# V's high part moved to ScalarE, the maximum turned in one pass, idle products, a tenth weight buffer and a new order of steps

## The chip, the core and the metric

The kernel runs on one core of a Trainium2 chip. The core has a matrix engine (TensorE, PE in the profile; its weight loads are PEld), three engines for elementwise work (VectorE is DVE, ScalarE is ACT, GpSimd is POOL) and SyncE (SP), which here only issues transfers. Every engine runs its own instructions strictly in the order in which they stand and waits for the others by semaphores. The metric is the device time of one launch in microseconds, as the median of several runs.

## The reference

Attention over 4 batches and 8 heads of 768 positions and 64 dimensions, in which a query sees the first 8 keys and the 96 keys up to itself, with a bias that falls linearly with the distance; then a soft mixture of 8 experts with 4 slots each over the 3072 resulting rows of 512.

```
scores = scale * q @ k.T + bias;  scores[~keep] = -1e9
a = softmax(scores);  x = (a @ v) as rows (B*S, H*D)
logits = x @ phi
slot_input = softmax(logits, over rows).T @ x
slot_out[e] = relu(slot_input[e] @ w1[e]) @ w2[e]
out = softmax(logits, over slots) @ slot_out
```

Everything is float32, and the weights w1 and w2 are 32 MB together.

## The kernel before

The attention is done in 16 units, numbered u: one pair of heads of one batch each. The keys of a unit stand in seven blocks of 120 (with the 8 global keys in front of each), and a block meets only the 216 queries that can see it. The code writes each stage of a unit as a small function, a step, and one long list, ORDER (line 51), says in which sequence the steps are issued. No scheduler comes after it: what ORDER gives is what every engine does in its queue. A step named `('w_lo', 3, 1, 2)` is w_lo of unit 3, head 1 of the pair, part 2.

The steps of a unit, with the lines of the kernel before:

- `load_qk` and `load_v` (L389, L392) fetch Q and K, and V. There are two buffers each.
- `scores(u, k)` (L518, PE) makes the products of Q and K in three parts, into two PSUM buffers sc used in turn; so a part can't start before the part two places ahead of it has been read.
- `biased(u, k)` (L527, DVE) reads such a part, adds the bias table and keeps the running maximum of each row.
- `max_t`, `max_r`, `max_b`, `max_c` (L534 PE, L537 DVE, L540 PE, L544 ACT) make one maximum of the unit out of the 128 of the rows and spread it again: a turn by a product with the identity, a reduction, a product, a copy.
- `exponential(u, i)` (L548, ACT) for the two heads i.
- `w_hi` (L551, ACT) rounds the weights to f16; `w_lo` in three parts (L558, POOL; a few as `w_lo_dve` on DVE) takes the difference to the rounded ones, also in f16. Each head has one buffer for them, so w_hi of the next unit waits until `values` of this one has read it.
- `v_hi` (L493, POOL) rounds V, scaled by 64, to f16, and `v_lo` (L500, DVE) makes the rest from V and v_hi.
- `values(u, i)` (L575, PE) makes 39 f16 products: high by high, high by low, low by high. It fills one half of the PSUM tile x.
- `ev_sums`, `ev_recs`, `ev_mul` (L588, L594, L600, DVE) divide by the row sums and free x; `tr` (L612, PE) turns the result and `tr_copy` (L617, ACT) copies it to SBUF; `logits` (L642, PE) follows after every second unit, and after every fourth the sums of the batch (`strip_...`, `by_token`, `dispatch`).

The bias table of the first pair is built by `table_even` and `table_odd` (L255 to L269, DVE), those of the other three by `table_pair` (L272, DVE). At the very start 12 products with a constant (L424) run on PE while nothing else can.

The weights come in 32 pieces of 1 MB. The first NW = 9 have buffers of their own and are loaded in the course of the attention (`piece`, and `extra` for parts of buffers that lie free). Thirteen more take the place of attention buffers as these fall free (`free`); the last ten are loaded once the first expert products have read theirs: five when the first half of the hidden products (L106) is issued, in halves, and five more in quarters. After the attention stand the last logits and sums, the hidden products (L106), their turning (L120), the combination weights (L170), the second products (L136, two output halves), and the combination (L196 to L202), which writes 12 times 512 KB.

## Time and profile before

| | |
|---|---|
| median of 3 runs | 218.66 us (218.41 to 218.75) |
| the profiled execution: its own time | 220.06 us |
| its span, from the first to the last instruction | 217.8 us |
| granted TensorE clock, mean | 0.933 |
| busy: PE, DVE, ACT, POOL | 183.6, 151.6, 121.4, 121.5 us |
| first `biased` starts | 10.04 us |
| `values` of unit 0, 2, 4, 12, first head, start | 27.87, 44.34, 59.25, 124.74 us |
| last `values` (unit 15, second head) ends | 151.34 us |
| last transfer to the output lands | 215.88 us |

The rows of a timeline read: start, duration, engine, line, operation, the tile written and the tiles read, and in brackets how long the engine had stood idle before and what ended that. A PE row covers several products, and its duration ends with the last of them; the next row starts some 0.07 to 0.16 us earlier than that, since products are pipelined.

### The profile page before, as it was taken

How to read it: one execution, taken by the hardware profiler on the slowest of the kernel's cores; microseconds unless marked ns; L12 is line 12 of the kernel's file. 1: busy time of each engine (PE TensorE's matmuls, PEld its weight loads, DVE VectorE, ACT ScalarE, POOL GpSimd, SP SyncE). 2: the span in 40 equal slices, each digit the busy share in tenths (PEclk: the TensorE clock that was granted, in tenths of full speed). 3: DMA queues.
4: the chain of work that ended last, by engine and by line, in shares of the span. 5: the costliest groups of instructions: out<-in, count | busy, mean ns of one | idle time of the engine just before them, and what ended most of it. 6: DMA issues, size and time to landing. Idle time of an engine off the chain costs nothing.

```text
span 217.8 us, 6430 instructions
## 1 busy us (share of the span) xinstructions
PE 183.6 (84%) x2644; PEld 135.3 (62%) x2644; DVE 151.6 (70%) x355; ACT 121.4 (56%) x169; POOL 121.5 (56%) x141
## 2 busy tenths in 40 slices
PE   8377799989898999998999998667899999899500
PEld 2155588878786787777787787456452366475500
DVE  4974759878878897988787997977367846151800
ACT  2008358598786786976886979962511653041500
POOL 7312929889999998898899799763000000000000
PEclk9955569999999999999999999999999999999965
DMA  4968429999998963755324657999985999979893
GB/s 149 414 248 307 161 86 354 377 377 399 389 385 311 343 232 125 242 175 196 120 75 169 225 166 246 416 381 389 369 331 178 409 409 387 386 270 342 280 339 123
DMA packets 21063, 61.40 MB, mean 282 GB/s; under 512 B 1952, under 2 KB 9376, under 8 KB 19488
## 3 DMA queue, kind: packets, MB, share of 16 engines
q1 hardware_dynamic: 20880, 60.89, 76.7%
q8 instruction: 23, 0.38, 0.7%
q14 instruction: 16, 0.13, 0.2%
q10 hardware_dynamic: 144, 0.00, 0.0%
HBM read 54.59 MB, written 6.29 MB: 280 GB/s over the span
## 4 chain that ended last, share of the span: by engine, by line
PE 41%; POOL 22%; DVE 15%; issue 10%; DMA 3%; ACT 3%; POOLq 0%; DVEq 0%; ACTq 0%; SPq 0%
POOL ph L558 20%; PE x L575 9%; PE x L136 7%; PE hp L106 6%; PE sc L518 6%; DVE ph L558 3%; DVE xn L600 2%; PE m L642 2%; PE m L612 2%; POOL v L493 2%; ACT ph L551 2%; DMA nraw<-in_n_dram 2%; DMA out_dram<-v 2%; DVE v L500 2%; PE ctp L170 2%
## 5 line engine op out<-in xcount | busy, mean ns | idle before, releaser
L558 POOL TENSOR_TENSOR ph<-tb,ph 128x432 f16<-128x432 f32 x91 | 101.4, 1147 | 21.5 <-ACT ph L551 21.1
L518 PE MATMUL sc<-raw 64*128 64x216 f32 (+2 forms) x448 | 53.6, 372 | 5.2 <-DVE mx L527 4.7
L551 ACT CAST ph<-tb 128x1296 f16<-128x1296 f32 x32 | 40.6, 1270 | 16.3 <-PE x L575 15.6
L575 PE MATMUL x<-v,ph 128*128 128x65 f16 (+1 forms) x1248 | 44.0, 195 | 6.5 <-DVE xmax L600 5.3
L518 PEld LDWEIGHTS sc<-raw 64*128 64x128 f32 x448 | 41.2, 206 | 13.0 <-DVE mx L527 6.2
L575 PEld LDWEIGHTS <-ph 128*128 128x128 f16 x1248 | 41.1, 98 | 12.5 <-issue 5.7
L548 ACT ACTIVATE tb<-tb,nb 128x1296 f32<-128x1296 f32 x32 | 43.5, 1375 | 0.3
L500 DVE SCALAR_TENSOR_TENSOR v<-vt,v 128x896 f16<-128x896 f32 x16 | 23.2, 1452 | 0.0
L527 DVE CUSTOM_DVE_ANT_1 tb<-sc,tt,mx 128x864 f32<-128x864 f32 x16 | 17.9, 1117 | 5.4 <-PE sc L518 4.8
L600 DVE CUSTOM_DVE_ANT_1 xn<-x,rc 120x448 f32<-120x448 f32 x32 | 18.9, 621 | 0.5
L493 POOL TENSOR_SCALAR v<-vt 128x896 f16<-128x896 f32 x16 | 15.7, 982 | 4.8 <-DVE mx L527 1.8
L612 PE MATMUL m<-ident,xn 120*128 120x120 f32 x105 | 15.4, 276 | 1.3 <-ACT xta L617 1.2
L544 ACT COPY nb<-m 128x1 f32<-128x1 f32 x16 | 2.6, 159 | 22.4 <-PE m L540 22.4
L612 PEld LDWEIGHTS m<-ident,xn 120*128 120x128 f32 x105 | 10.7, 141 | 3.5 <-ACT xta L617 1.4
L527 DVE CUSTOM_DVE_ANT_1 tb<-sc,tt 128x864 f32<-128x864 f32 x8 | 8.5, 1058 | 5.2 <-PE sc L518 4.8
L527 DVE CUSTOM_DVE_ANT_1 tb<-sc,xta,mx 128x864 f32<-128x864 f32 x8 | 8.9, 1118 | 2.4 <-PE sc L518 2.0
L106 PE MATMUL hp<-wp,sl 128*32 128x512 f32 x72 | 10.5, 594 | 0.0
L199 ACT COPY ph<-cp 128x512 f32<-128x512 f32 x8 | 4.1, 595 | 10.9 <-PE cp L196 10.9
L527 DVE CUSTOM_DVE_ANT_1 tb<-sc,xtt,mx 128x864 f32<-128x864 f32 x8 | 8.9, 1116 | 1.2 <-POOL v L493 0.6
L534 PE MATMUL m<-ident,mx 128*1 128x128 f32 x32 | 6.5, 286 | 2.5 <-DVE mx L527 2.5
L136 PE MATMUL x<-wp,tb 128*32 128x256 f32 x96 | 7.5, 381 | 1.1 <-DVE flag L858 1.1
L540 PEld LDWEIGHTS m<-mm,bsel 2*128 2x128 f32 x32 | 5.1, 198 | 4.8 <-DVE mm L537 1.2
(196 smaller groups left out, 272.3 us busy)
## 6 DMA issues: line engine op xcount, KB each, us to landing
raw<-in_qk_dram SPq DMA_DIRECT2D x15, 832.0 KB, 4.9
wp<-in_w_dram SPq DMA_DIRECT2D x9, 1024.0 KB, 9.2
vt<-in_v_dram SPq DMA_DIRECT2D x16, 448.0 KB, 4.7
wp<-in_w_dram SPq DMA_DIRECT2D x10, 512.0 KB, 7.5
out_dram<-ph SPq DMA_DIRECT2D x8, 512.0 KB, 5.2
tb<-in_w_dram SPq DMA_DIRECT2D x3, 1024.0 KB, 7.1
raw<-in_w_dram SPq DMA_DIRECT2D x8, 256.0 KB, 5.4
out_dram<-v SPq DMA_DIRECT2D x4, 512.0 KB, 6.1
```

The source lines that it names most:

```text
L106: nc.tensor.matmul(out=hp[n][32 * s:32 * s + 32, :], lhsT=slv(a, c, s), rhs=w1(e, c // 2)[:, (c % 2) * DF + 512 * n:(c % 2) * DF + 512 * n ...
L136: nc.tensor.matmul(out=o[32 * s:32 * s + 32, 0:w], lhsT=ht[:, c, 32 * s:32 * s + 32], rhs=w2(4 * a + s, half)[:, c0 + c * w:c0 + c * w + w ...
L493: nc.gpsimd.tensor_scalar(out=vhi[u % 2][:, :, :, 0:D], in0=vraw[u % 2], scalar1=V_SC, scalar2=0.0, op0=ALU.mult, op1=ALU.add)
L500: nc.vector.scalar_tensor_tensor(out=vlo[k].rearrange("p j i d -> p (j i) d"), in0=vraw[k].rearrange("p j i d -> p (j i) d"), scalar=V_SC, ...
L518: nc.tensor.matmul(out=z[:, i, at:at + n], lhsT=r_[r, KCOL[j]:KCOL[j] + KR], rhs=r_[r, KW + KB * j:KW + KB * j + n], start=True, stop=True)
L527: nc.vector.tensor_tensor_reduce(out=tb(u)[:, :, BW * k:BW * k + BW], in0=sc[(3 * u + k) % 2][:, :, 0:BW], in1=table.unit(u % NP, k), scal ...
L548: nc.scalar.activation(out=t, in_=t, func=AF.Exp, bias=nbs[u], scale=T_SC)
L551: nc.scalar.copy(out=blocks(phi_[i])[:, :, 0:QW], in_=tb(u)[:, i].rearrange("p (s c) -> p s c", c=QW))
L558: (engine or nc.gpsimd).tensor_tensor(out=blocks(plo_[i])[:, c, 0:QW], in0=tb(u)[:, i].rearrange("p (s c) -> p s c", c=QW)[:, c], in1=bloc ...
L575: nc.tensor.matmul(out=x[:, (D + 1) * t:(D + 1) * t + d], lhsT=w[:, c:c + P], rhs=vv[:, j, i, 0:d], start=(z == 0), stop=(z == len(ops) - ...
L600: nc.vector.tensor_tensor_reduce(out=xnb[(u // 2) % 3][:, :, c:c + D], in0=xv[:, i, :, 0:D], in1=rcs.pop((u, i)).unsqueeze(2).to_broadcast ...
L612: nc.tensor.transpose(out=m[:, at:at + KB], in_=xnb[(u // 2) % 3][:, t, P * (p % 2):P * (p % 2) + P], identity=ident[0:KB, 0:KB])
```

## The change

Five things change.

1. In 12 of the 16 units (all but 4, 7, 8 and 13) the step `v_hi` is replaced by `v_hi_act`, which does the same rounding on ScalarE: `nc.scalar.activation(out=vhi, in_=vraw, func=AF.Copy, scale=V_SC)`. The function stood in the kernel before and was not used.
2. `max_t` is a transpose of the column of 128 maxima (one pass of the array over the identity) in place of a product with the identity in float32.
3. A step `warm(u, count)` makes `count` products of a constant of ones with 512 columns, into the first row of x, which nobody reads. ORDER holds two: 7 after the scores (0, 1), and 10 after `max_b` of unit 0.
4. NW is 10. The tenth piece is loaded in the course of the attention, and of the ten late pieces nine remain (five in halves, four in quarters).
5. ORDER is another sequence throughout. Four `tr_copy` (of units 0, 5, 9 and 10) go to DVE, and four parts of w_lo in place of five: one of unit 9, three of unit 15, and none of unit 14.

```diff
-NW = 9
+NW = 10
-ORDER = [('load_qk0', 0), ('load_phis', 0), ('load_qk', 0), ('load_v', 0), ('keys', 0), ('load_qk', 1), ...
+ORDER = [('load_qk0', 0), ('load_qk', 0), ('load_v', 0), ('load_qk', 1), ('keys', 0), ('load_v', 1), ...
...
+    def warm(u, count):
+        for _ in range(count):
+            nc.tensor.matmul(out=xx[0:1, 0], lhsT=busy_in[:, 0:1], rhs=busy_in, start=True, stop=True)
...
     def max_t(u):
         ms[u, "m"] = m = bank(("max", u))
-        nc.tensor.matmul(out=m[0:1, 0:P], lhsT=mxs.pop(u)[:, 2:3], rhs=ident, start=True, stop=True)
+        nc.tensor.transpose(out=m[0:1, 0:P], in_=mxs.pop(u)[:, 2:3], identity=ident)
```

From the `warm` function on, the lines of the changed kernel stand four further down: the scores are L522 there, the maximum's turn L538, w_lo L562, the values L579.

The queue of PE from the first scores on, before. (sc_171 and sc_172 are the two score buffers, raw_92 and raw_93 Q and K of units 0 and 1.)

```order
L518 MATMUL sc_171<-raw_92 128x216 x4
L518 MATMUL sc_172<-raw_92 128x216 x4
L518 MATMUL sc_171<-raw_92 128x216 x2
L518 MATMUL sc_171<-raw_92 128x168 x2
L518 MATMUL sc_171<-raw_92 128x48 x2
L534 MATMUL m<-ident,mx 1x128
L518 MATMUL sc_171<-raw_93 128x216 x4
L540 MATMUL m<-mm_160,bsel 128x1
L518 MATMUL sc_172<-raw_93 128x216 x6
L518 MATMUL sc_172<-raw_93 128x168 x2
```

The same place now (all buffer numbers are higher by one; the weight loads of the idle products are left out, and their row L511, which stands seven times, is shown once):

```order
L522 MATMUL sc_172<-raw_93 128x216 x4
L522 MATMUL sc_173<-raw_93 128x216 x4
L511 MATMUL x<-const-bfloat16-1.0 1x512
L522 MATMUL sc_172<-raw_93 128x216 x2
L522 MATMUL sc_172<-raw_93 128x168 x2
L522 MATMUL sc_172<-raw_93 128x48 x2
L522 MATMUL sc_173<-raw_94 128x216 x4
L538 MATMUL m<-ident,mx 1x128
L522 MATMUL sc_172<-raw_94 128x216 x4
L544 MATMUL m<-mm_161,bsel 128x1
```

The first part of unit 1's scores now stands ahead of unit 0's maximum, and the seven idle products fill the place between the second and the third part of unit 0; ten more follow behind the last row shown.

The queue of POOL from its last constant to unit 2's second head, before (v_99 is V's f16 tile, ph_97 and ph_98 the weights' of the two heads):

```order
L443 MEMSET sl 128x280
L493 TENSOR_SCALAR v_99<-vt 128x14x64 x2
L558 TENSOR_TENSOR ph_97<-tb_94,ph_97 128x2x216 x3
L558 TENSOR_TENSOR ph_98<-tb_94,ph_98 128x2x216 x3
L558 TENSOR_TENSOR ph_97<-tb_95,ph_97 128x2x216 x3
L558 TENSOR_TENSOR ph_98<-tb_95,ph_98 128x2x216 x3
L493 TENSOR_SCALAR v_99<-vt 128x14x64
L558 TENSOR_TENSOR ph_97<-tb_96,ph_97 128x2x216 x3
L558 TENSOR_TENSOR ph_98<-tb_96,ph_98 128x2x216 x3
```

And now, to the second head of unit 3:

```order
L443 MEMSET sl 128x280
L562 TENSOR_TENSOR ph_98<-tb_95,ph_98 128x2x216 x3
L562 TENSOR_TENSOR ph_99<-tb_95,ph_99 128x2x216 x3
L562 TENSOR_TENSOR ph_98<-tb_96,ph_98 128x2x216 x3
L562 TENSOR_TENSOR ph_99<-tb_96,ph_99 128x2x216 x3
L562 TENSOR_TENSOR ph_98<-tb_97,ph_98 128x2x216 x3
L562 TENSOR_TENSOR ph_99<-tb_97,ph_99 128x2x216 x3
L562 TENSOR_TENSOR ph_98<-tb_95,ph_98 128x2x216 x3
L493 TENSOR_SCALAR v_100<-vt 128x14x64
L562 TENSOR_TENSOR ph_99<-tb_95,ph_99 128x2x216 x3
```

The first rounding of V left on POOL is that of unit 4. On ScalarE the queue now begins like this (L548 to L555 are L544 to L551 of before):

```order
L496 ACTIVATE v_100<-vt 128x14x64 x2
L548 COPY nb<-m 128x1
L552 ACTIVATE tb_95<-tb_95,nb 128x1296
L555 CAST ph_98<-tb_95 128x6x216
L552 ACTIVATE tb_95<-tb_95,nb 128x1296
L555 CAST ph_99<-tb_95 128x6x216
L548 COPY nb<-m 128x1
L552 ACTIVATE tb_96<-tb_96,nb 128x1296
L555 CAST ph_98<-tb_96 128x6x216
```

Two roundings of V stand ahead of the first exponential. Those of the later units stand mostly between the first exponential of a unit and its first rounding L555.

## The prediction

> **What bounds the kernel now.** I read the page first, then busy time by stage, the groups of instructions, and the timeline of the places that the stages point to. The page:

> ```profile
> span 217.8 us, 6430 instructions
> PE 183.6 (84%) x2644; PEld 135.3 (62%) x2644; DVE 151.6 (70%) x355; ACT 121.4 (56%) x169; POOL 121.5 (56%) x141
> PEclk9955569999999999999999999999999999999965
> ```

> The shares are means over stages of different kinds, and the clock row shows half speed in slices 3 to 5. So I cut the span where the clock changes and at values of units 2, 4 and 12 and the end of unit 15:

> ```profile
> core 0: us, PE busy (x) PEld busy (x) DVE busy (x) ACT busy (x) POOL busy (x), PEclk, DMA share, GB/s
> 4.26:11.09 6.83, 2.90 (x21) 1.54 (x19) 6.10 (x20) 0.00 (x0) 3.04 (x12) 1.00 1.04 405
> 11.09:31.57 20.48, 16.69 (x113) 12.99 (x115) 12.70 (x22) 9.43 (x9) 7.97 (x7) 0.50 0.59 209
> 31.57:44.34 12.77, 11.90 (x194) 10.05 (x193) 11.15 (x27) 8.03 (x10) 11.93 (x12) 1.00 0.89 331
> 44.34:59.25 14.91, 14.28 (x250) 12.15 (x251) 12.01 (x29) 12.33 (x17) 14.29 (x14) 1.00 0.99 392
> 59.25:124.74 65.49, 63.03 (x1053) 50.55 (x1053) 55.48 (x127) 51.68 (x70) 60.03 (x57) 1.00 0.63 217
> 124.74:151.34 26.60, 20.78 (x428) 17.68 (x429) 22.08 (x48) 18.82 (x24) 20.86 (x20) 1.00 0.86 321
> 151.34:217.80 66.46, 50.50 (x585) 29.20 (x584) 30.39 (x82) 19.60 (x40) 0.00 (x0) 0.93 0.88 318
> ```

> Four things are to be seen. From 11.09 to 31.57 us the clock is at 0.50 and POOL has only 7.97 us of work in 20.48. From 44.34 to 124.74 (ten units, 8.04 us each) PE is busy 77.3 of 80.4 us, so PE is the bound there and POOL (74.3) is close behind it. From 124.74 on no engine is full: a chain through all of them sets the pace. The last stage has nothing of the attention in it. The stage at half clock in the timeline:

> ```profile
> 0.77 4.46 PE L424 MATMUL wp<-const-bfloat16-1.0 128*1 128x512 bf16 x12 [0.77 <-PEq L1105]
> 6.63 1.00 PE L518 MATMUL sc<-raw 64*128 64x216 f32 x8 [0.47 <-DMA raw<-in_qk_dram]
> 8.00 1.35 POOL L493 TENSOR_SCALAR v<-vt 128x896 f16<-128x896 f32 x1 [1.71 <-DMA vt<-in_v_dram]
> 8.25 0.25 DVE L259 COPY tt<-xn 128x432 bf16<-128x432 bf16 x1
> 8.43 1.05 DVE L261 COPY tt<-xn 128x168 bf16<-128x168 bf16 x2
> 10.04 1.06 DVE L527 CUSTOM_DVE_ANT_1 tb<-sc,tt 128x864 f32<-128x864 f32 x1
> 11.16 1.95 PE L518 MATMUL sc<-raw 64*128 64x216 f32 x12 [3.53 <-DVE mx L527]
> 14.95 1.81 PE L518 MATMUL sc<-raw 64*128 64x216 f32 x8
> 15.33 1.07 DVE L500 SCALAR_TENSOR_TENSOR v<-vt,v 128x896 f16<-128x896 f32 x1
> 19.06 1.06 DVE L527 CUSTOM_DVE_ANT_1 tb<-sc,tt 128x864 f32<-128x864 f32 x1 [2.65 <-PE sc L518]
> 20.25 7.03 POOL L558 TENSOR_TENSOR ph<-tb,ph 128x432 f16<-128x432 f32 x6 [8.15 <-ACT ph L551]
> 27.87 2.31 PE L575 MATMUL x<-v,ph 128*128 128x65 f16 x39
> 31.59 6.20 POOL L558 TENSOR_TENSOR ph<-tb,ph 128x432 f16<-128x432 f32 x6 [4.31 <-ACT ph L551]
> 31.82 1.36 PE L575 MATMUL x<-v,ph 128*128 128x65 f16 x39
> ```

> PE stood idle for 3.53 us, from 7.63 to 11.16, and the clock fell at 11.09. From then the same eight score products take 1.81 us instead of 1.00, and DVE waits for them. Values of unit 0 come at 27.87 although POOL had the first head's three of its six parts done near 23.3: they stand behind scores of unit 2 in PE's queue.

> **The change part by part.** The prices, by group:

> ```profile
> L558 POOL TENSOR_TENSOR ph<-tb,ph 128x432 f16<-128x432 f32 x91 | 101.4, 1147 | 21.5 <-ACT ph L551 21.1 <-PE sc L518 0.3
> L548 ACT ACTIVATE tb<-tb,nb 128x1296 f32<-128x1296 f32 x32 | 43.5, 1375 | 0.3
> L551 ACT CAST ph<-tb 128x1296 f16<-128x1296 f32 x32 | 40.6, 1270 | 16.3 <-PE x L575 15.6 <-POOL ph L558 0.3
> L500 DVE SCALAR_TENSOR_TENSOR v<-vt,v 128x896 f16<-128x896 f32 x16 | 23.2, 1452 | 0.0
> L493 POOL TENSOR_SCALAR v<-vt 128x896 f16<-128x896 f32 x16 | 15.7, 982 | 4.8 <-DVE mx L527 1.8 <-DMA vt<-in_v_dram 1.7 <-PE x L575 1.2
> L534 PE MATMUL m<-ident,mx 128*1 128x128 f32 x32 | 6.5, 286 | 2.5 <-DVE mx L527 2.5
> L617 ACT COPY xtt<-m 128x480 f32<-128x480 f32 x5 | 2.8, 558 | 0.7 <-PE m L612 0.7
> L136 PE MATMUL x<-wp,tb 128*32 128x256 f32 x96 | 7.5, 381 | 1.1 <-DVE flag L858 1.1
> L459 ACT ACT_TABLE_LOAD x1 | 1.3, 1283 | 1.2 <-PEq L1105 1.2
> raw<-in_qk_dram SPq DMA_DIRECT2D x15, 832.0 KB, 4.9
> ```

> *V's high part.* POOL loses 12 x 0.98 = 11.8 us (L493). ScalarE's price for 896 elements to f16 is in no row; it lies between 0.56 (480 elements, L617) and 1.27 (1296, L551), and the line through both gives 0.92, which I take: 12 x 0.92 = 11.0 us more on ACT. In the ten units from 44.34 ACT was busy 64.0 of 80.4 us; seven of the twelve fall there, so it goes to 70.4, and POOL to about 67. Neither is then the bound; PE is, so in these units the move itself is worth little. Behind a `v_hi_act` in ACT's queue stands w_hi, for which POOL waits; it is covered as long as w_hi waits for values of the unit before anyway, as it did for 15.6 us in all (L551).

> *The start.* In 8.00 to 9.35 POOL rounds V, and a DVE copy of 168 elements and one of 48 together take 1.05 us, where the one of 432 before took 0.25. With POOL empty I take 0.25 for both: the first `biased` moves from 10.04 to 9.2. (The bound the other way is no gain, 10.04.) [...]

> Now I follow the queues with full-clock prices (scores 1.00, values 1.36, exponential 1.38, rounding 1.27, w_lo 1.0, six in 6.20, `biased` 1.1). The seven idle products lie at 7.6 to 9.1 (12 of them took 4.46 us, mostly at half clock, so 0.43 each then and 0.21 at full); that leaves PE idle for only 1.2 us until the third part, at 10.3. Biased of unit 0 ends at 12.6; v_lo stands ahead of `max_r` (1.07 us, into 13.6); turn, `max_b` and copy lead to the exponential at 14.5; rounding at 15.9, w_lo from 17.2 to 20.1. The ten idle products (14.3 to 16.5) end before the scores behind them can start, since these wait for `biased` of unit 1 (17.1). Values of unit 0 start at 20.6 (before 27.87), w_lo of unit 1 at 25.1 (31.59). Going on in this way, PE, POOL and ACT each taking over from the other, I get values of unit 2 at 35.5 (44.34), of unit 3 at 42.2 (51.95), and of unit 4 at 51.0 where it was 59.25. **Term: -8.3 us.** With the clock at half from 11.09 on all the same, the scores cost 1.81 and 1.95, the ten idle products 4.3 (15.8 to 20.1) and hold up the scores behind them: values of unit 0 come at 25.9, and the gain is 2.0; this is the lower bound.

> *Transfers at the start.* Q and K of units 0 and 1 are issued no later than before; those of unit 3 wait for the third scores of unit 1 (end at 18.2) and land 4.9 us later by the median, at 23.1, just in time for the 23.3 of the walk. A piece of 1 MB takes 2.6 us at the 405 GB/s of the stages' first row; none stands between these two, and if an earlier one still runs, unit 3 starts up to 2.6 us later, once.

> *The maximum's turn.* Two passes per unit become one. The rows:

> ```profile
> 56.93 0.38 PE L534 MATMUL m<-ident,mx 128*1 128x128 f32 x2
> 57.24 1.08 PE L518 MATMUL sc<-raw 64*128 64x216 f32 x12
> 59.25 0.93 PE L575 MATMUL x<-v,ph 128*128 128x65 f16 x25 [0.63 <-DVE xmax L600]
> 124.74 1.35 PE L575 MATMUL x<-v,ph 128*128 128x65 f16 x39 [0.26 <-DVE xmax L600]
> 149.99 1.35 PE L575 MATMUL x<-v,ph 128*128 128x65 f16 x39 [1.30 <-DVE xmax L600]
> ```

> The pair's records take 0.38 us, one takes 0.286 by the group, so 0.1 us per unit leaves PE's time: 0.9 us in units 4 to 12 (bounds 0, if the weight load sets the pace, and 0.19).

> *Units 4 to 12* then need 63.0 - 0.9 = 62.1 us of PE, against 65.5 us now. With POOL 6 us lighter some of the 2.5 us of PE idle time should close; I take 0.6 of it. **Term: -1.5** (bounds -3.4, PE without a gap, and +2, the idle time doubled by ACT's fuller queue).

> *Units 12 to 15.* PE is busy 20.8 of 26.6 us. POOL loses two roundings of V (2.0 us; that of unit 13 stays) and gets the two parts of w_lo of unit 14 that DVE had (2.3 us). DVE is freed of these, and the logits of unit 13 and turns of units 13 and 14 move ahead of the last values, off the path behind them; that is counted here too. **Term: -2** (bounds -5.8, no idle time, and +1).

> *The tenth buffer* saves 1 MB of late loads, 2.6 us of transfer. PE's only idle time before the second products (L136) is one of 1.1 us for a flag, none for a weight, so it is worth 0; the last writes could gain up to 0.5. The rest after 151.34 is the same work, shifted; its cover is that loads into freed buffers come relative to the attention's end as now.

> **Sum** against the profiled execution's own time: 220.06 - 8.3 - 1.5 - 2.0 = 208.3 us; span 217.8 - 11.8 = 206.0. The median of the runs is 1.4 us below that execution, so the forecast is 218.66 - 11.8 = **206.9 us**.

> **The rivals.**

> *The clock falls anyway.* The idle products leave gaps of 1 to 2 us, and fill under half of 7.67 to 11.09. For: from 11.09 to 31.57 PE was busy 81% of the time (16.69 of 20.48) and the clock didn't come back, and no stage kept it with less than 78% (20.78 of 26.60) but the first, at whose end it fell. Against: it fell only after a stretch with not one product, and idle times of up to 1.30 us after 124.74 did nothing. Then the start gives 2 to 3 us: 218.66 - 2.5 - 1.5 - 2 = 212.7. [...]

> *The later units give the start back.* ACT's queue is full in order, with V's rounding ahead of w_hi, and by the sums above every engine is at 83% or more; if idle time on PE grows from 4% to 9% over units 4 to 12 (+3.5) and units 12 to 15 gain nothing: 218.66 - 8.3 + 3.5 = 213.9. For: w_hi is what POOL waited for, 21.1 us. Against: ACT's waits for PE show it ahead, not behind.

> *Slower.* One mechanism: each `v_hi_act` delays w_hi, and with it w_lo and values, by its whole 0.92 us, because in the new order w_hi no longer waits for values. Twelve times is 11.0 us; it decides as soon as the start gives less than that, as with the clock at half: 218.66 - 2.5 + 11.0 - 2 = 225.2. Against: 15.6 us of waits before w_hi now.

> *It doesn't do what it says*: a change of ACT's function table before each copy of another kind. Copies, casts and exponentials alternate in this trace with one table load (L459), so I give it no weight.

> **How the numbers follow.** Forecast 0.62, clock 0.17, given back 0.12, slower 0.07, another 0.02. The forecast's own spread comes from the bounds of its three terms: 202 (terms -9, -3, -4.5) to 211. The clock rival covers 210 to 215.5. The range of 201.5 to 215.0 leaves out the slower case and the ends of the others, about 0.18. A change within 0.2% (0.44 us) can't be told from none; only the cases at the edge between given back and slower fall there, 0.02. Faster 0.91, slower 0.07.

> **What would show it.** Right: full clock from before 11 us to the end, or half for under 7 us; values of unit 0 at 20 to 22 and of unit 4 at 50 to 53; V's rounding on ACT at 0.9; one L538 record per unit; PE busy over 95% from unit 4 to unit 12; the stage behind the last values 65 to 66.5 us long. Wrong: a half clock up to 20 us and beyond; w_hi without a wait before it and POOL waiting for it in every unit; PE idle over 5 us in units 4 to 12; PE waiting for Q and K or for a weight.

## The result, and the profile after

The changed kernel takes **211.41 us** (median of four runs, 210.70 to 212.97) against 218.70 us before on the same chip (four runs, 218.41 to 219.71): ratio 0.967, 95% interval 0.961 to 0.973. It is 7.3 us faster where 11.8 were forecast; the range of 201.5 to 215.0 us holds it. The execution that was profiled is the shortest of the four, 210.70 us, with a span of 208.9.

The page of the changed kernel:

```profile
span 208.9 us, 6433 instructions
PE 180.1 (86%) x2645; PEld 131.2 (63%) x2645; DVE 145.4 (70%) x358; ACT 129.5 (62%) x177; POOL 105.2 (50%) x130
...
PEclk9999999999999999999999999969999999999955
```

The clock row has no half speed at the start any more, but it has a dent in slice 27. The busy time by stage, cut at values of units 0, 2, 4 and 12 and at the end of the last values, and below it two windows of 3.41 us from the end of the attention:

```profile
core 0: us, PE busy (x) PEld busy (x) DVE busy (x) ACT busy (x) POOL busy (x), PEclk, DMA share, GB/s
4.31:11.14 6.83, 5.00 (x34) 2.54 (x33) 5.68 (x21) 1.12 (x2) 1.65 (x11) 1.00 1.04 414
11.14:21.18 10.04, 8.55 (x69) 5.27 (x65) 9.56 (x18) 6.14 (x6) 3.41 (x4) 1.00 0.95 366
21.18:36.29 15.11, 13.90 (x242) 12.15 (x240) 12.36 (x28) 12.06 (x14) 11.71 (x13) 1.00 1.01 388
36.29:52.59 16.30, 15.21 (x258) 12.70 (x257) 12.89 (x31) 15.00 (x19) 15.77 (x15) 1.00 0.99 381
52.59:114.36 61.77, 60.34 (x1039) 49.54 (x1036) 53.25 (x130) 54.22 (x72) 50.18 (x50) 1.00 0.62 227
114.36:142.77 28.41, 24.13 (x451) 19.69 (x450) 19.62 (x46) 21.48 (x30) 19.03 (x18) 0.94 0.87 315
142.77:208.90 66.13, 49.40 (x562) 28.16 (x561) 30.39 (x82) 18.03 (x36) 0.00 (x0) 0.92 0.83 297
...
134.02:137.43 3.41, 1.26 (x36) 1.04 (x33) 2.11 (x7) 3.33 (x4) 3.07 (x3) 1.00 1.01 384
137.43:140.85 3.42, 3.42 (x53) 2.47 (x49) 1.94 (x2) 0.88 (x2) 1.43 (x1) 0.50 1.02 427
```

Read against the same stages before, the difference has four parts. Values of unit 4 come at 52.59 instead of 59.25 (-6.7). Units 4 to 12 take 61.77 instead of 65.49 (-3.7), with PE busy for all but 1.4 us. Units 12 to 15, up to the end of the last values, take 28.41 instead of 26.60 (**+1.8**): here part of the gain is lost, in a stage in which the clock was at half for one window. The rest takes 66.13 instead of 66.46. Groups of its page, with the count, the busy time, the mean ns of one, and the idle time before them:

```profile
L562 POOL TENSOR_TENSOR ph<-tb,ph 128x432 f16<-128x432 f32 x92 | 96.6, 1081 | 33.1 <-ACT ph L555 27.7
...
L500 DVE SCALAR_TENSOR_TENSOR v<-vt,v 128x896 f16<-128x896 f32 x16 | 19.8, 1238 | 1.1 <-ACT v L496 1.0
...
L496 ACT ACTIVATE v<-vt 128x896 f16<-128x896 f32 x12 | 11.3, 944 | 7.4 <-DMA vt<-in_v_dram 7.4
```

V's rounding takes 0.944 us on ScalarE (L496). And two groups that nobody edited became cheaper: V's low part on DVE (L500) fell from 1.452 to 1.238 us each, W's low part on POOL (L562) from 1.147 to 1.081. The experiment with V all on POOL, below, shows that both are dearer again when POOL has more to do (1.655 and 1.103 us each in units 4 to 12, against 1.328 and 1.065 in the changed kernel).

### The profile page after: what moved, and what is told of

It is laid out like the page before. It is cut to its first block, busy times and chain, and to the rows that moved or that the text cites. A ratio compares the mean times of both kernels' runs of the same rounds, so it can differ in the third digit from the quotient of the medians.

```text
span 208.9 us, 6433 instructions
## 1 busy us (share of the span) xinstructions
PE 180.1 (86%) x2645; PEld 131.2 (63%) x2645; DVE 145.4 (70%) x358; ACT 129.5 (62%) x177; POOL 105.2 (50%) x130
## 5 line engine op out<-in xcount | busy, mean ns | idle before, releaser
L562 POOL TENSOR_TENSOR ph<-tb,ph 128x432 f16<-128x432 f32 x92 | 96.6, 1081 | 33.1 <-ACT ph L555 27.7
L522 PE MATMUL sc<-raw 64*128 64x216 f32 (+2 forms) x448 | 48.3, 343 | 3.9 <-DVE mx L531 3.4
L555 ACT CAST ph<-tb 128x1296 f16<-128x1296 f32 x32 | 40.7, 1271 | 9.5 <-PE x L579 8.4
L579 PE MATMUL x<-v,ph 128*128 128x65 f16 (+1 forms) x1248 | 43.6, 194 | 2.7 <-DVE xmax L604 2.2
L579 PEld LDWEIGHTS <-ph 128*128 128x128 f16 x1248 | 40.9, 98 | 7.0 <-issue 5.6
L522 PEld LDWEIGHTS sc<-raw 64*128 64x128 f32 x448 | 36.6, 186 | 10.0 <-DVE mx L531 5.0
L500 DVE SCALAR_TENSOR_TENSOR v<-vt,v 128x896 f16<-128x896 f32 x16 | 19.8, 1238 | 1.1 <-ACT v L496 1.0
L616 PE MATMUL m<-ident,xn 120*128 120x120 f32 x105 | 14.8, 273 | 2.4 <-DVE xmax L604 1.0
L496 ACT ACTIVATE v<-vt 128x896 f16<-128x896 f32 x12 | 11.3, 944 | 7.4 <-DMA vt<-in_v_dram 7.4
L136 PE MATMUL x<-wp,tb 128*32 128x256 f32 x112 | 10.9, 381 | 1.1 <-DVE flag L862 1.1
L199 ACT COPY ph<-cp 128x512 f32<-128x512 f32 x4 | 2.1, 590 | 10.9 <-PE cp L196 10.9
L136 PEld LDWEIGHTS x<-wp,tb 128*32 128x32 f32 x112 | 5.5, 110 | 3.8 <-DVE flag L862 1.2
L181 DVE TENSOR_SCALAR ohs<-x,sgn 128x256 fp32r<-128x256 f32 x2 | 1.0, 484 | 9.4 <-PE ft L861 4.9
L548 ACT COPY nb<-m 128x1 f32<-128x1 f32 x16 | 2.5, 157 | 7.7 <-PE m L544 7.6
## 6 DMA issues: line engine op xcount, KB each, us to landing
raw<-in_qk_dram SPq DMA_DIRECT2D x15, 832.0 KB, 6.3
```

The costliest lines, as they stand in the source:

```text
L136: nc.tensor.matmul(out=o[32 * s:32 * s + 32, 0:w], lhsT=ht[:, c, 32 * s:32 * s + 32], rhs=w2(4 * a + s, half)[:, c0 + c * w:c0 + c * w + w ...
L496: nc.scalar.activation(out=vhi[u % 2][:, :, :, 0:D], in_=vraw[u % 2], func=AF.Copy, scale=V_SC)
L500: nc.vector.scalar_tensor_tensor(out=vlo[k].rearrange("p j i d -> p (j i) d"), in0=vraw[k].rearrange("p j i d -> p (j i) d"), scalar=V_SC, ...
L522: nc.tensor.matmul(out=z[:, i, at:at + n], lhsT=r_[r, KCOL[j]:KCOL[j] + KR], rhs=r_[r, KW + KB * j:KW + KB * j + n], start=True, stop=True)
L555: nc.scalar.copy(out=blocks(phi_[i])[:, :, 0:QW], in_=tb(u)[:, i].rearrange("p (s c) -> p s c", c=QW))
L562: (engine or nc.gpsimd).tensor_tensor(out=blocks(plo_[i])[:, c, 0:QW], in0=tb(u)[:, i].rearrange("p (s c) -> p s c", c=QW)[:, c], in1=bloc ...
```

## The experiments

Each experiment was timed beside the kernel before on one chip; on those chips that kernel took 219.7 to 220.2 us (218.70 on the chip of the result), so a time is read with its ratio. The stages below are from each profiled execution, cut as above; the stage from unit 4 to unit 12 repeats to within 0.3 us wherever it was not touched.

| kernel | values of unit 4 | units 4 to 12 | unit 12 to the last values' end | the rest |
|---|---|---|---|---|
| before | 59.25 | 65.49 | 26.60 | 66.46 |
| changed | 52.59 | 61.77 | 28.41 | 66.13 |
| changed, no idle products | 52.75 | 61.78 | 28.40 | 66.37 |
| changed, without the ten | 54.06 | 61.79 | 26.84 | 66.31 |
| changed, V all on POOL | 53.33 | 64.51 | 29.06 | 66.30 |
| changed, maximum in two passes | 52.92 | 62.78 | 28.29 | 66.61 |
| new order alone | 55.24 | 65.20 | 30.24 | 66.38 |
| before, with idle products | 57.43 | 65.49 | 26.59 | 67.09 |
| before, V on ScalarE | 58.44 | 66.20 | 28.43 | 66.83 |
| changed, clock held at the end | 52.87 | 62.05 | 26.85 | 66.23 |
| and the eviction first | 53.00 | 61.78 | 26.42 | 65.60 |

### The idle products

```diff
-('warm', 0, 7),
...
-('warm', 0, 10),
```

> The changed kernel without its 17 idle products (7 and 10); all else as changed. Theory: the clock is held by them. In the changed kernel PE was busy 61% of the window from 7.72 to 11.14 us; without seven products of 0.21 us it is 18%, so the clock falls to 0.5 at about 11.1 and stays there to 25 or later; values of unit 4 come at 57 to 59 instead of 52.6, and the kernel takes 216 to 218 us (211.4 + 4.5 to 6.5). Rival: the new order and the empty POOL earn the start by themselves; then unit 4 stays at 52 to 54 and the time at 211 to 213.

Measured: 211.17 us (four runs, 211.14 to 212.79), ratio 0.961, interval 0.953 to 0.969. The theory called the fall of the clock right and its price wrong. Busy time in this kernel's first windows of 3.41 us, and from values of unit 0 to values of unit 4 (columns as above):

```profile
7.83:11.24 3.41, 0.63 (x8) 0.59 (x8) 3.04 (x11) 1.06 (x2) 0.00 (x0) 1.00 1.03 416
11.24:14.65 3.41, 3.41 (x23) 2.59 (x21) 3.17 (x7) 0.85 (x1) 0.00 (x0) 0.50 0.90 319
14.65:18.06 3.41, 1.38 (x14) 1.03 (x12) 3.24 (x6) 2.36 (x3) 0.00 (x0) 1.00 1.02 411
18.06:21.48 3.42, 3.42 (x23) 2.64 (x21) 2.59 (x5) 2.99 (x3) 2.90 (x4) 0.50 0.93 321
22.14:52.75 30.61, 29.11 (x496) 24.85 (x495) 25.33 (x58) 26.95 (x32) 27.46 (x27) 1.00 1.00 391
```

The clock fell at 11.24 and at 18.06, but it was back one window later each time; in the new order PE's work filled those windows (3.41 of 3.41 us). Values of unit 0 came 0.96 us later than with the idle products, those of unit 4 only 0.16 later. So the idle products were not what the start's 6.7 us came from. How much of it comes from the clock coming back after one window, where the kernel before stayed at half for 20.5 us, this run doesn't separate.

```diff
-('warm', 0, 10),
```

> The changed kernel with the first seven idle products and without the ten of unit 0. Theory: the window from 14.55 to 17.96 us, busy 86% in the changed kernel, has about 25% without the ten, less than the 37% after which the clock fell at 137.43; so it falls to 0.5 at 17.96 and comes back 3.4 to 10 us later; values of unit 4 at 54 to 57, the time 213 to 216 us. Rival: only a window without any product lowers the clock early in the program, and the ten are idle ballast; then unit 4 stays at 52 to 53 and the time at 211 to 212, or gains some tenths.

Measured: 211.64 us (210.50 to 213.27), ratio 0.962, interval 0.953 to 0.971. The clock went as the theory said: the window from 14.89 had PE busy for 0.77 us, and half speed followed from 18.30 to 25.13; values of unit 4 at 54.06. This costs 1.5 us, more than leaving out all seventeen, since here the two half windows lie on values of unit 0. The time didn't follow, because the end did not lose its window: there PE was busy 63% of the window that decided, where it had been 37%. The three windows of this kernel's start:

```profile
14.89:18.30 3.41, 0.77 (x10) 0.78 (x12) 3.24 (x5) 3.35 (x4) 0.52 (x1) 1.00 1.02 417
18.30:21.71 3.41, 3.38 (x20) 2.41 (x19) 2.62 (x7) 1.96 (x2) 3.41 (x5) 0.50 0.92 325
21.71:25.13 3.42, 3.42 (x47) 2.80 (x43) 1.84 (x5) 0.00 (x0) 1.91 (x2) 0.50 0.89 327
```

And the kernel before, with idle products added:

```diff
 ('scores', 0, 1),
+('warm', 0, 10),
...
+('warm', 0, 10),
 ('scores', 1, 2),
```

> The kernel before with ten idle products after the second scores of unit 0 and ten ahead of the third scores of unit 1; nothing else of the change. Theory: the clock holds, the scores of units 0 to 2 take 1.0 us instead of 1.8, and values of unit 4 come 4 to 6 us earlier than 59.25, the time is 213 to 215 us: most of what the whole change gained. Rival: the start is bound by the waits between engines and POOL's late first rounding, not by the clock; then unit 4 gains 1 to 2 us and the time is 217 to 218.

Measured: 216.64 us (214.10 to 218.77), ratio 0.979, interval 0.970 to 0.989. In the profiled execution unit 4 gained 1.8 us, as the rival had it. The clock still fell once there (half from 13.99 to 20.81, after a window that was 31% busy), a third of the half time before. But this execution is the longest of the four, 218.77 us with a mean clock of 0.958. The others took 216.34 (0.968), 216.95 (0.973) and 214.10 (0.978), and the last lies in the theory's range, 5.8 us under the 219.92 of the kernel before on this chip. It left no trace, so it is not shown where its time went. The clock's share of the old start is about 1.8 us at least, then, and may be several times that; in the old order a held clock could gain much of what the new order gains.

### V's high part, the order, and the maximum

```diff
-('v_hi_act', 0),
+('v_hi', 0),
...
-('v_hi_act', 15),
+('v_hi', 15),
```

> The changed kernel with V's high part of all 16 pairs on POOL again, at the same places of the order. Theory A, the order alone: POOL has 11 us more to do but was idle 33 us before its parts of W's low half, so unit 4 stays within 0.5 us of 52.6 and the time within 1 us of 211.4. Theory B, the move of V: POOL's rounding collides with DVE's table copies (the first biased scores go from 9.5 to 10.0) and stands ahead of W's low parts in a POOL that is 59% to 97% busy; unit 4 comes 1 to 2 us later, units 4 to 12 grow by 1 to 3 (61.8 to 63 to 65), the time is 213 to 216.

Measured: 216.14 us (215.26 to 218.71), ratio 0.983, interval 0.972 to 0.994. By the stages of the table **4.3 us of the gain are gone** when V goes back to POOL (0.7, 2.7, 0.7 and 0.2). At the start a DVE cast beside POOL's rounding (L257) takes 0.99 us instead of 0.26 and the first `biased` comes at 10.24 instead of 9.51; the clock also fell there, for one window from 11.81, although all seventeen idle products were in place, so the 0.7 may not be the move's alone. Of the 4.3 us, 2.7 lie in units 4 to 12, where I had called the move worth little. The busy time of this stage:

```profile
53.33:117.84 64.51, 60.74 (x1039) 49.53 (x1037) 55.99 (x130) 50.30 (x66) 58.48 (x57) 1.00 0.60 220
```

Three groups of the same stage:

```profile
L562 POOL TENSOR_TENSOR ph<-tb,ph 128x432 f16<-128x432 f32 x48 | 51.6, 1103 | 6.0 <-ACT ph L555 5.7 <-DVE xmax L604 0.3
...
L579 PE MATMUL x<-v,ph 128*128 128x65 f16 (+1 forms) x624 | 21.6, 193 | 1.2 <-POOL ph L562 1.2
...
L500 DVE SCALAR_TENSOR_TENSOR v<-vt,v 128x896 f16<-128x896 f32 x8 | 13.2, 1655 | 1.2 <-POOL v L493 1.2
```

PE's work is the same to 0.4 us (60.74 against 60.34), but its idle time grows from 1.43 to 3.77 us, and values wait 1.2 us for POOL. POOL is busy 58.48 of 64.51 us instead of 50.18 of 61.77. Of these 8.3 us, 5.6 are V's rounding in the six pairs that moved (0.94 each); the rest is one low part more in the stage and collisions: a low part of W takes 1.103 us on the mean instead of 1.065, and V's low part on DVE 1.655 instead of 1.328.

```diff
-('v_hi', 0),
+('v_hi_act', 0),
...
-('v_hi', 15),
+('v_hi_act', 15),
```

> The kernel before with V's high part of the same 12 pairs on ScalarE, its order kept. Theory A, the order: the move alone does little, 0 to -1 us (unit 4 at 58 to 59.3, units 4 to 12 at 64.5 to 65.5). Theory B, the move: -2 to -4 us, above all in units 4 to 12 (62 to 63.5), since POOL was 92% busy there. A loss (+1 to +3) where the rounding on ScalarE stands ahead of the rounding of W in an order not made for it.

Measured: 221.67 us (ten runs, 220.91 to 222.91), ratio 1.010, interval 1.006 to 1.013. The same move in the old order **loses** 2 us. By the stages of the table it gains 0.8 up to unit 4, loses 0.7 in units 4 to 12, 1.8 in units 12 to 15 and 0.4 in the rest; the 1.8 hold one window at half clock, from 141.78. The waits of units 4 to 12 show what happens there at full clock; before, the first row read 5.1 us:

```profile
POOL ph L558 <- ACT ph L551: 10.2, 6, 3.4
DVE v L500 <- ACT v L496: 1.9, 2, 1.3
PE x L575 <- POOL ph L558: 1.4, 2, 1.2
```

POOL has less to do and waits twice as long for ACT's rounding of W, in whose queue V's rounding now stands too. That is the mechanism of the prediction's slower rival, at 0.7 us in eight units.

```diff
-NW = 10
+NW = 9
...
-('v_hi_act', 0),
+('v_hi', 0),
...
-('warm', 0, 7),
...
-('warm', 0, 10),
...
-('piece', 9),
...
-        nc.tensor.transpose(out=m[0:1, 0:P], in_=mxs.pop(u)[:, 2:3], identity=ident)
+        nc.tensor.matmul(out=m[0:1, 0:P], lhsT=mxs.pop(u)[:, 2:3], rhs=ident, start=True, stop=True)
```

> The new order alone: V's high part on POOL in all pairs, no idle products, the maximum in two passes, nine weight buffers (the tenth piece is then loaded with the late ones). Theory A: the order is most of the gain: unit 4 at 52.5 to 54, the time 212 to 214 us, 5 to 7 under the kernel before. Theory B, the parts count: 215 to 218, the order by itself worth 1 to 4.

Measured: 218.37 us (ten runs, 215.71 to 220.04), ratio 0.991, interval 0.986 to 0.997. The new order alone is worth about 2 us by the ratio. Its executions differ by 4.3 us, the shortest two (215.71 and 215.76) at a mean clock of 0.952; the profiled one took 219.0 at 0.940, with 10.2 us at half clock before 23.73. In it the order brings unit 4 to 55.24 (-4.0), does next to nothing in units 4 to 12 (65.20 against 65.49, both at full clock), and its units 12 to 15 are 3.6 us longer than before, with the clock at half for two windows:

```profile
120.44:150.68 30.24, 25.59 (x453) 20.92 (x452) 20.61 (x46) 19.77 (x28) 20.56 (x20) 0.89 0.86 314
```

So its first and last stage are those of an execution that the clock made longer. In units 4 to 12 neither the order nor V's move pays by itself: the order alone gives 0.3 us, the move alone costs 0.7, and both together with the turn give 3.7.

```diff
-        nc.tensor.transpose(out=m[0:1, 0:P], in_=mxs.pop(u)[:, 2:3], identity=ident)
+        nc.tensor.matmul(out=m[0:1, 0:P], lhsT=mxs.pop(u)[:, 2:3], rhs=ident, start=True, stop=True)
```

> The changed kernel with the maximum turned by a float32 product of two passes, as before. Theory: 0.1 us of PE per unit, 16 units, 12 of them on PE's path: units 4 to 12 at 62.4 to 62.8 instead of 61.8, the time +0.5 to +1.5. Rival: the maximum is also on the chain from scores to exponential, and the second pass adds more in the first and the last units: +1.5 to +3. Or nothing: the turn hides beside weight loads.

Measured: 212.56 us (211.35 to 214.41), ratio 0.968, interval 0.958 to 0.978. Units 4 to 12 grow by 1.0 us, PE's busy time in them by 1.2. The turn costs what the theory said, about 0.12 us per unit, over eight units. The busy time of this stage:

```profile
52.92:115.70 62.78, 61.50 (x1048) 49.96 (x1045) 53.29 (x130) 54.49 (x72) 50.33 (x50) 1.00 0.60 221
```

### The end of the attention

PE at the end, in the timeline of the changed kernel (start, duration, operation, and in brackets the idle time before it):

```profile
133.51 0.86 PE L579 MATMUL x<-v,ph 128*128 128x65 f16 x23
134.75 0.67 PE L579 MATMUL x<-v,ph 128*128 128x65 f16 x16 [0.38 <-POOL ph L562]
137.19 2.12 PE L579 MATMUL x<-v,ph 128*128 128x65 f16 x39 [1.77 <-DVE xmax L604]
139.25 0.62 PE L646 MATMUL m<-xta,phis 128*32 128x240 f32 x5
...
140.95 0.63 PE L616 MATMUL m<-ident,xn 120*128 120x120 f32 x4
141.42 1.35 PE L579 MATMUL x<-v,ph 128*128 128x65 f16 x39
```

Values of unit 15 wait 1.77 us for the eviction of unit 14; the window around that wait is 37% busy (1.26 of 3.41 us), and in the next one the same 39 products take 2.12 us instead of 1.35. Behind them stand the logits and a turn that the new order put ahead of the last values.

```diff
 ('values', 14, 1),
+('hold', 0, 7),
...
+    def hold(u, count):
+        for _ in range(count):
+            nc.tensor.matmul(out=sc[1][0:1, 0], lhsT=busy_in[:, 0:1], rhs=busy_in, start=True, stop=True)
```

> The changed kernel with seven more idle products behind the second values of unit 14, where PE stood idle from 135.42 to 137.19 us, written to a bank of scores that is no longer read. Theory: the clock fell to 0.5 from 137.43 to 140.84 because the window before was busy only 37%; with the products it is about 80%, the clock holds, the last values end at 141.4 to 141.7 instead of 142.77 and the time is 1.0 to 1.4 us less than the changed kernel's (210.0 to 210.4). Rival: the fall has another cause than PE's idle time (power, a transfer), or the products hold up the values behind them; then the window stays at 0.5 or the end does not move, 211.4 or more.

Measured: 210.12 us (209.74 to 211.63), ratio 0.956, interval 0.948 to 0.964. The clock stays full, and the stage shrinks from 28.41 to 26.85 us, by 1.6. The kernel without the ten idle products, whose clock held there by itself, has the same 26.84. So **1.6 of the 1.8 us that this stage lost are the clock**. The two windows, in this kernel:

```profile
134.06:137.47 3.41, 3.02 (x48) 1.79 (x46) 1.89 (x6) 3.26 (x5) 3.12 (x4) 1.00 1.01 364
137.47:140.88 3.41, 3.26 (x75) 2.71 (x75) 2.17 (x4) 2.08 (x5) 1.91 (x2) 1.00 1.02 420
```

What is left is a chain. In the changed kernel DVE takes the strip's maximum (L680) ahead of the eviction of unit 12 (L592), and POOL waits for what follows from it. Its timeline:

```profile
122.05 0.92 DVE L680 TENSOR_TENSOR state<-al,state 128x1 f32<-128x1 f32 x1
...
123.07 0.16 DVE L592 TENSOR_TENSOR rsall<-x,eps 120x14 f32<-120x14 f32 x1
...
124.90 2.52 PE L579 MATMUL x<-v,ph 128*128 128x65 f16 x78 [0.42 <-DVE xmax L604]
...
127.67 2.94 POOL L562 TENSOR_TENSOR ph<-tb,ph 128x432 f16<-128x432 f32 x3 [3.76 <-ACT ph L555]
```

```diff
-('strip_max', 11), ('max_b', 14), ('ev_sums', 12), ('free', 1), ('strip_exp', 11), ('ev_recs', 12), ('w_lo', 13, 1, 0), ('ev_mul', 12, 0), ('max_c', 14), ('by_token', 11), ('exponential', 14, 0), ('strip_sum', 11), ('ev_mul', 12, 1),
+('max_b', 14), ('ev_sums', 12), ('free', 1), ('ev_recs', 12), ('w_lo', 13, 1, 0), ('ev_mul', 12, 0), ('max_c', 14), ('exponential', 14, 0), ('ev_mul', 12, 1), ('strip_max', 11),
...
+('strip_exp', 11), ('biased', 15, 1), ('strip_sum', 11), ('free', 3), ('values', 13, 1), ('w_hi', 14, 0), ('by_token', 11),
...
 ('values', 14, 1),
+('hold', 0, 7),
```

> The changed kernel with the seven idle products behind the second values of unit 14, and in units 12 and 13 one thing moved: the eviction of unit 12 now stands on DVE ahead of the strip's maximum, the exponential of unit 14 on ACT ahead of the strip's, and the turn by token on PE behind the second values of unit 13. Theory: in the changed kernel the strip's maximum (0.92 us on DVE beside POOL, 0.15 alone) and the strip's exponential held up the eviction, and with it values of unit 13 and the rounding for unit 14, for which POOL then waited 3.76 us; values of unit 13 come 0.9 to 1.2 us sooner after values of unit 12 (9.4 to 9.7 us instead of 10.54), POOL's wait falls to about 2.6, and the last values end 0.7 to 1.2 us sooner than with the products alone: 209.0 to 209.4. Rival: the end is set by what follows (POOL's queue of low parts, ACT's queue of unit 15), the gain is lost by unit 15: 209.9 to 210.3.

Measured: 208.87 us (208.62 to 210.74), ratio 0.952, interval 0.945 to 0.960. Values of unit 13 come 9.41 us after those of unit 12 instead of 10.54, and POOL's wait is 2.60 us, both as the theory said; the strip's maximum, now taken when POOL is nearly done, needs 0.31 us. By the last values 0.4 us of it is left (26.42 against 26.85): in between values of unit 14 wait for the eviction of unit 13, which stands behind the dispatch. So the rival has half of it. Of the 1.2 us by which this profiled execution is shorter than that with the products alone, 0.6 lie in the rest (65.60 against 66.23), which the edit doesn't touch; why is open. The same places in this kernel's timeline (its lines stand four further down):

```profile
122.47 0.17 DVE L596 TENSOR_TENSOR rsall<-x,eps 120x14 f32<-120x14 f32 x1
...
124.05 0.31 DVE L684 TENSOR_TENSOR state<-al,state 128x1 f32<-128x1 f32 x1
...
124.19 2.52 PE L583 MATMUL x<-v,ph 128*128 128x65 f16 x78 [0.82 <-DVE xmax L608]
...
126.95 2.94 POOL L566 TENSOR_TENSOR ph<-tb,ph 128x432 f16<-128x432 f32 x3 [2.60 <-DVE v L500]
```

Two attempts went further in the same stage.

```diff
-('v_lo', 14), ('tr', 12, 1), ('by_token_copy', 11), ('biased', 15, 2), ('w_lo', 14, 0, 0), ('free', 9), ('tr_copy', 12, 1), ('dispatch', 11), ('exponential', 14, 1),
+('v_lo', 14), ('exponential', 14, 1), ('tr', 12, 1), ('lnat_copy', 11), ('by_token_copy', 11), ('biased', 15, 2), ('w_lo', 14, 0, 0), ('free', 9), ('tr_copy', 12, 1), ('max_t', 15),
...
+('values', 14, 0), ('exponential', 15, 0), ('dispatch', 11), ('w_lo', 14, 1, 0), ('v_hi_act', 15), ('w_lo', 14, 1, 1), ('v_lo', 15), ('w_hi', 15, 0),
...
+('values', 14, 1), ('exponential', 15, 1), ('tr', 12, 0), ('tr_copy', 12, 0), ('free', 10), ('tr', 13, 0), ('tr', 13, 1),
```

> No idle products at the end; the steps from the maximum of unit 14 to values of unit 15 in another order: as in the run beside it, and ACT's exponential of unit 15 right behind the rounding of unit 14, V's rounding of unit 15 behind that, the turn by dispatch on PE between the two values of unit 14, the turns of units 12 and 13 behind them, where PE stood idle. Theory: ACT's order was what unit 15 waited for; the last values end at 139 to 140.5 instead of 142.77, the clock holds since the turns fill PE's idle time, and the time is 207.5 to 209 us. Rival: POOL's low parts of units 14 and 15 (12 of about 1.0 to 1.4 us) are the bound there; then the end gains only what POOL gains at its start, 1 us, and the clock may fall again: 209.5 to 210.5.

Measured: 212.79 us (209.59 to 213.94), ratio 0.959, interval 0.948 to 0.970. It missed. The clock fell again at 134.99, after a window that was 33% busy, and ACT waited 2.00 us for a turn whose copy I had put ahead of the rounding of W. The profiled execution is a long one, 213.94 us, and shows something else too: at its start the clock fell at 12.11 and at 25.76 us, although all seventeen idle products were there. Values of unit 1 came at 34.61. Windows of this start:

```profile
8.70:12.11 3.41, 1.91 (x18) 1.21 (x17) 2.92 (x9) 1.01 (x2) 0.00 (x0) 1.00 1.04 419
...
22.35:25.76 3.41, 1.91 (x34) 1.72 (x30) 2.14 (x5) 2.35 (x3) 2.84 (x3) 1.00 0.94 320
25.76:32.59 6.83, 6.04 (x57) 4.72 (x57) 2.73 (x8) 3.01 (x3) 3.51 (x4) 0.50 0.99 388
```

```diff
-('ev_mul', 13, 1), ('w_lo', 14, 0, 1), ('w_hi', 14, 1), ('max_t', 15), ('dispatch_sum', 11), ('free', 17), ('max_r', 15), ('tr', 12, 0), ('ev_mul', 13, 0), ('v_hi_act', 15), ('w_lo', 14, 1, 0), ('max_b', 15), ('values', 14, 0), ('max_c', 15),
+('ev_mul', 13, 1), ('ev_mul', 13, 0), ('w_lo', 14, 0, 1), ('w_hi', 14, 1), ('max_t', 15), ('max_r', 15), ('max_b', 15), ('max_c', 15), ('values', 14, 0), ('dispatch_sum', 11), ('free', 17), ('exponential', 15, 0), ('tr', 12, 0), ('w_lo', 14, 1, 0), ('v_hi_act', 15), ('w_lo', 14, 1, 1), ('tr_copy_dve', 12, 0), ('v_lo', 15),
...
+('values', 14, 1), ('tr', 13, 0), ('tr', 13, 1), ('hold', 0, 3),
```

> On top of the run with the eviction of unit 12 moved ahead: on DVE the eviction of unit 13 and the reduction of unit 15's maximum ahead of the addition of the dispatch (they waited for it, 130.6 us), on ACT the exponential of unit 15 ahead of V's rounding, one turn copy on DVE instead of ACT, the turns of unit 13 on PE behind the second values of unit 14 with three idle products behind them instead of seven. Theory: values of unit 14 come 0.7 to 0.9 us sooner and the last values end at 140.2 to 140.6 instead of 141.2; time 208.0 to 208.5 us against 208.87. Rival: POOL's low parts set unit 15, or the clock falls because of fewer products: 208.9 to 210.5.

Measured: 210.25 us (six runs, 209.22 to 211.91), ratio 0.956, interval 0.952 to 0.961. Values of unit 14 come 15.93 us after those of unit 12, 0.85 sooner than in the run it builds on, as the theory said; the last values end 26.96 after them, 0.5 later. DVE lost it, where V's low part and one of W's low parts, both beside POOL, stand ahead of the eviction of unit 14. Values of unit 14 were done at 135.98; the eviction began at 137.47. This execution also lost 1.4 us at the start (values of unit 4 at 54.44 against 53.00), where the clock fell at 25.87, although the start was not edited. DVE in this kernel's timeline:

```profile
134.72 1.50 DVE L500 SCALAR_TENSOR_TENSOR v<-vt,v 128x896 f16<-128x896 f32 x1
136.13 1.41 DVE L566 TENSOR_TENSOR ph<-tb,ph 128x432 f16<-128x432 f32 x1
137.47 0.16 DVE L596 TENSOR_TENSOR rsall<-x,eps 120x14 f32<-120x14 f32 x1
```

Last, the start again, on top of the kernel with the eviction first; `warm1` is `warm`, written to the bank half of the second head's values:

```diff
-('warm', 0, 7),
+('warm', 0, 11),
...
+('warm1', 0, 4),
 ('scores', 3, 0),
```

> On top of the same run: eleven instead of seven idle products in the first gap and four more ahead of the first scores of unit 3, where PE stood idle for 1.2 us. Theory: the executions of one kernel differ by 2 us because the window of 3.41 us over which the clock is decided starts at another point each time; windows of the start that were 56% busy were followed by a half clock in another run (12.11 and 25.76 us, values of unit 1 at 34.6 instead of 30.8), windows of 60 to 68% were not. With no window under 75% the late executions are gone: all within 0.6 us of the fastest, 208.3 to 208.9, with a mean clock of 0.978 or more in each. Rival: the spread comes from something else (the late loads of weights, the end); then one in four executions stays 1.5 to 2.5 us longer, as before.

Measured: 209.00 us (six runs, 208.05 to 209.70), ratio 0.951, interval 0.948 to 0.954. No execution is 2 us late any more, but they differ by 1.65 us, not by 0.6, and the two slowest have clocks of 0.973 and 0.980; part of the spread is something else, which stays open. This kernel and the one it builds on are the fastest of the study; the intervals of both ratios lie below that of the changed kernel.

## Why the prediction was right, and where it was wrong

**The start (-8.3 forecast, -6.7 measured).** Its times held to within 0.8 us up to unit 2: values of unit 0 at 21.18 (20.6), W's low part of unit 1 at 25.87 (25.1), values of unit 2 at 36.29 (35.5). Then unit 3 came at 43.92 (42.2) and unit 4 at 52.59 (51.0), so the carrying on "in this way" was too smooth by 1.6 us in all. What failed is the price of the clock: "with the clock at half from 11.09 on all the same" the gain was to be 2.0. That case, with the idle products in and the clock at half for long, stands in no run; but without the idle products the clock did fall, and the gain was 6.5. The step took it that the clock stays at half about as long as in the kernel before; it came back after one window each time. The order by itself accounts for 4.0 of the 6.7; V's move (0.7), the turn (0.3) and the idle products (0.2) are what each costs when it is taken back. The 1.5 us left over may come from the parts together, or from the clock, which was at half for 10.2 us of the start in the run of the order alone; the runs don't separate these. That the 1.05 us of table copies fall to 0.27 when POOL is empty, and the first `biased` moves to 9.51 (9.2 forecast), was right.

**Units 4 to 12 (-1.5 forecast, -3.7 measured).** The turn was right: 0.9 forecast, 1.0 measured. The step that failed is "so in these units the move itself is worth little", because "PE is" the bound. It is worth 2.7 us there. In the new order PE stands idle for 3.77 us with V on POOL and for 1.43 with V on ScalarE, so a bound engine at 94% to 96% still had something to gain from POOL being on time; and POOL's busy time was not a fixed cost that one subtracts from, since its collisions with DVE go with it. Against the kernel before, PE's idle time there fell from 2.46 to 1.43 us and its busy time from 63.03 to 60.34. About 1 us of the latter is the turn, and another 1.0 is no gain: the new order issues five turns of results behind values of unit 12 (51 instead of 56 in this stage, 27 instead of 20 in the next). I had the two prices in front of me (V's low part at 1.45 us on average where the first took 1.07) and didn't use them. In the kernel before, the changed one and the one with V all on POOL, V's low part takes 1.07 to 1.09 us with POOL idle and 1.14 to 1.96 with POOL busy all through it, a low part of W 0.60 to 1.42 on DVE and 0.99 to 1.88 on POOL: either engine's instruction was up to about 0.9 us longer beside the other's.

**Units 12 to 15 (-2 forecast, +1.8 measured).** This term had the wrong sign. The clock of one window took 1.6 us, for which the sum, made with full-clock prices, had no place (half "for under 7 us" was among its signs of being right); it had weighed the clock's fall only at the start. And the logits and turns that moved ahead of the last values were counted as gain "off the path behind them". They were hidden behind the last eviction before, and the rest shrank by only 0.33 us; in front of the last values they are on the path: the last low parts of unit 15 ended at 139.98 us, and its last values began at 141.42, behind the logits and a turn. The turns that came over from units 4 to 12 lie in this stage too.

**The rest** (65 to 66.5 forecast) took 66.13. **The tenth buffer**, at 0, was not tried alone: the rest takes 65.6 to 66.6 us in the kernels with ten buffers and 66.4 to 67.1 in the four with nine, which differ in more than that.

**The median.** Of the 4.5 us by which the forecast missed, 2.1 come from the step that carried over "1.4 us below that execution": the changed kernel's profiled execution lies 0.7 us under its median, not above it. Against its own profiled execution the sum missed by 2.4 (208.3 against 210.7). That it came so near is partly luck: the start missed by +1.6, units 4 to 12 by -2.2, units 12 to 15 by +3.8 and the rest by -0.3, and these offset each other. The forecast's own spread ended at 211; the range held 211.41 because it was drawn over the rivals too.

**The rivals.** Two of them, at 212.7 and 213.9, came nearer to the measured time than the forecast's 206.9, neither by its own mechanism alone. "The clock falls anyway" was right about the clock's weakness and wrong about the place and the price. "The later units give the start back" is half true: the end gave back 1.8, but units 4 to 12 gained. The slower rival's mechanism is real, as the old order with V on ScalarE shows (+0.7 us in units 4 to 12). In the new order POOL waits 7.7 us for ACT's rounding in these units, more than the 5.1 before, but this no longer reaches PE: values waited 1.4 us for POOL in the old order with V on ScalarE, and in the changed kernel PE stood idle ahead of them for 0.1 us in all.

## What to carry to other kernels

Before a move between engines is called worthless because another engine is the bound, look at what the bound engine's idle time waits for and at whether the relieved engine's instructions are slowed by collisions (here by up to 0.9 us each): both can come back. Test an order and the placement that it was made for together, since in units 4 to 12 each alone gave next to nothing or a loss. And go through all windows in which PE is less than about 60% busy (here every fall of the clock came after one of at most 56%), at the end as well as at the start, before a sum assumes a full clock.

## What the runs showed of the hardware

```profile
22.46:25.87 3.41, 1.81 (x21) 1.70 (x20) 1.79 (x3) 2.87 (x4) 1.52 (x2) 1.00 0.99 352
25.87:29.28 3.41, 3.41 (x49) 2.62 (x46) 1.07 (x2) 1.31 (x2) 2.94 (x3) 0.50 1.01 403
```

The second is the window of the seven idle products in the changed kernel, 61% busy, after which the clock stayed full:

```profile
7.72:11.14 3.42, 2.08 (x13) 0.93 (x13) 3.05 (x11) 1.12 (x2) 0.00 (x0) 1.00 1.04 420
```

The window ahead of a fall need not be empty. It was in the kernel before, from 7.67 to 11.09 us; other falls came after windows that were 18% to 56% busy and whose longest gap was 1.0 to 2.8 us (37% and 1.77 us in the changed kernel). The percentages rest on the profile's modelled ends of matmuls, so the border is that of this measure.

**Coming back takes a full window.** Of the windows at half clock with work in them, the nine that were under 80% busy were all followed by another; of those at 95% or more nineteen were followed by full speed and five were not. What tells the five apart is open. The kernel before stayed at half for 20.5 us in this way: three of its six windows were 59% to 66% busy.

**One place, several outcomes.** The windows start at another point in each execution, and the same gap cost nothing, one window or two: with the same steps up to unit 4, the profiled execution of the changed kernel (windows counted from 0.90 us after its first instruction) lost no window there, that of the second attempt on the end of the attention (from 1.98 us) one, from 25.87 us, and that of the first (from 1.87 us) three, from 12.11 and, two, from 25.76 us. This fits executions of one kernel that are 2 us apart; the experiment with a fuller start removed the latest ones but not all of the spread.
